# TensorE as hardware loops, with weight tiles picked by register and one semaphore for each kind of weight load

## The chip, the cores and the metric

The kernel runs on one core of a Trainium2 chip. The metric is device time in microseconds (us) of one execution. Each time below is a median of several executions. Every experiment was timed beside the kernel before, on the same chip and in the same rounds. A ratio is the mean time of one kernel's fast runs over the mean of the other's fast runs in the same rounds, so it is not quite the ratio of the quoted medians.

The engines are TensorE (PE, with weight loads as PEld), VectorE (DVE), ScalarE (ACT), GpSimd (POOL) and the sync engine that issues the loads (SP). A *unit* is one head of one batch: 128 units in all, each with a 3 MB tile of K and a 3 MB tile of V.

## The reference, cut to what matters

Two independent attention blocks decode one token against a cache, and their outputs are concatenated:

```python
B, Sq, D, H, Sk, Dh = 2, 1, 640, 32, 8192, 192          # for blocks A and B
q = (x @ wq).reshape(B, Sq, H, Dh).transpose(0, 2, 1, 3)
scores = einsum("bhqd,bhkd->bhqk", q, k_cache) * Dh ** -0.5
o = einsum("bhqk,bhkd->bhqd", softmax(scores), v_cache)
out = o.transpose(0, 2, 1, 3).reshape(B, Sq, H * Dh) @ wo
```

Everything is bfloat16. The caches make 805 MB of the 837 MB that are read, and each byte is used once.

## The kernel before

Each engine has a list of operations, each with the events it waits for. An operation stands in a *slot*, roughly the unit it belongs to. The emitter writes the list out, or, for a range of slots that repeats, as a hardware loop whose waits are computed from the turn number:

```python
lo, period, n = loop                 # slots lo .. lo + period * n - 1, as n turns
...
for fn, need, has_sig, _ in plan[:where[0]]:          # written out before the loop
    self.put(eng, fn, need, has_sig)
with eng.Fori(0, n) as i:                             # the loop
    for fn, need, has_sig, _ in body:
        self.put(eng, fn, [(sem, i * step[id(sem)] + val) for sem, val in need], has_sig)
for fn, need, has_sig, _ in plan[where[-1] + 1:]:     # written out after it
    self.put(eng, fn, need, has_sig)
```

Only VectorE and ScalarE loop, 15 turns of 8 units each; TensorE is written out in full:

```python
LOOPS = {"dve": (6, 8, 15), "act": (6, 8, 15)} if NU == 128 else {"dve": None, "act": None}
```

The loads wait for buffers. K and V have two tiles each; a K tile is free when VectorE has multiplied it, a V tile when TensorE has used it:

```python
S_sp.add(sp_k(u), waits=[key("d1b", u - NK)])         # NK = 2
S_sp.add(sp_v(u), waits=[key("pv", u - NV)])          # NV = 2
```

For each unit VectorE multiplies K by the query and sums three quarters of the products; ScalarE sums the other quarter, in 16 activations with an accumulator:

```python
for t in range(na_of(u)):                              # 16 per unit
    put(act_tab, u, 10 + t, act_acc(u, t), w, ...)
```

TensorE's work in a unit is 32 matmuls of probabilities with V. Of every four units, two add a query projection with `wq` and one an output projection with `wo`.

## Time and profile before

1972.22 us, median of 3 runs (1970.92 to 1972.57).

| Quantity | Value | View |
|---|---|---|
| Span of the profiled run | 1970.0 us | first line of the page |
| TensorE matmuls / VectorE / ScalarE busy | 57% / 84% / 46% | page, part 1 |
| Data moved | 837.52 MB | page, part 3 |
| Rate from 100 to 450 us and from 600 to 1800 us | 430 and 430 GB/s | table of stretches |
| Issue to landing of a 3 MB tile | 22.4 to 24.0 us | page, part 6 |

The page's part 2 cuts the span into 40 slices. These are the busy tenths of the 16 DMA engines, averaged over them, and the rate:

```profile
DMA  9999999999999999999999999999999999999996
GB/s 386 431 428 432 430 428 432 428 429 431 427 433 431 428 430 428 432 431 429 430 430 430 429 430 430 429 431 428 431 430 429 431 429 430 430 430 431 429 430 279
```

The DMA is full from start to tail: digit 9 in 39 of 40 slices. Part 3 lists the DMA queues: packets, MB, share of 16 engines' span.

```profile
q1 hardware_dynamic: 55856, 836.79, 99.5%
q8 instruction: 39, 0.64, 0.1%
q14 instruction: 11, 0.09, 0.0%
```

The data are q1. The other two are marked as instructions, so they are read as fetches of the engines' own programs: q8 as TensorE's (39 packets of 16 KB here), q14 as that of other engines (11 packets of 8 KB here).

Part 5 gives busy time, mean ns of one, idle time just before and what ended most of it:

```profile
L376 PE MATMUL ops<-vb,pb 128*33 128x384 bf16 x4096 | 957.5, 409 | 842.1 <-DMA vb<-in_A_v_cache_dram 364.2
...
L279 DVE TENSOR_TENSOR prodA<-kb,qbc 128x3072 bf16<-128x3072 bf16 x128 | 226.1, 1766 | 262.8 <-DMA kb<-in_B_k_cache_dram 130.2
```

Both compute engines wait for data: TensorE for V (689.0 of the 842.1 us, by the list of waits over both blocks), VectorE for K. Part 6 gives, for each kind of load, its count, KB of one and median us from issue to landing:

```profile
vb<-in_A_v_cache_dram SPq DMA_DIRECT2D x64, 3072.0 KB, 22.9
kb<-in_A_k_cache_dram SPq DMA_DIRECT2D x63, 3072.0 KB, 24.0
kb<-in_B_k_cache_dram SPq DMA_DIRECT2D x63, 3072.0 KB, 22.7
vb<-in_B_v_cache_dram SPq DMA_DIRECT2D x62, 3072.0 KB, 22.4
```

At 430 GB/s a tile takes 7.3 us, so about three tiles are under way at any time.

The trace also records each landing event: 16 separate increments of the semaphore for every 3 MB tile. The profile counts 16 DMA engines, so each increment is read here as one engine's share landing; the events carry no engine number, and this reading is the author's. The time from a tile's first increment to its last is called its *spread* below.

### The profile page before, as it was taken

Reading aid. Unit: us, or ns where it says so; the run is one execution under the profiler, and the core shown is the slowest. Engines: PE = TensorE matmul, PEld = TensorE weight load, DVE = VectorE, ACT = ScalarE, POOL = GpSimd, SP = SyncE. Lnnn points to the kernel's source line nnn. Section 1 sums busy time; section 2 is a strip of 40 time slices with the busy share of each in tenths; the row PEclk is TensorE's granted clock in tenths of the full one; section 3 lists DMA queues with packets and bytes.
Section 4 is the critical chain, followed back from the end, with each engine's and each line's share of the span. In section 5 each row is a group of like instructions: output and inputs, shape, how many; then the busy total and the mean of one; then the engine's idle time right before and its main releaser. Section 6 shows DMA issues by size and latency. Waiting matters only on the chain.

```text
span 1970.0 us, 18081 instructions
## 1 busy us (share of the span) xinstructions
PE 1118.6 (57%) x5014; PEld 593.7 (30%) x5014; DVE 1655.3 (84%) x962; ACT 904.7 (46%) x4763; POOL 113.8 (6%) x270
## 2 busy tenths in 40 slices
PE   2565556555555565555654655556655565555657
PEld 1233223323232333223332333223332233222324
DVE  7887888888888888888888888888788888888886
ACT  4444444544445444454445444444444444544454
POOL 3000000000000000000000000000000000000001
PEclk9777777777777777777777777777777777777778
DMA  9999999999999999999999999999999999999996
GB/s 386 431 428 432 430 428 432 428 429 431 427 433 431 428 430 428 432 431 429 430 430 430 429 430 430 429 431 428 431 430 429 431 429 430 430 430 431 429 430 279
DMA packets 55922, 837.52 MB, mean 425 GB/s; under 512 B 7352, under 2 KB 18240, under 8 KB 22976
## 3 DMA queue, kind: packets, MB, share of 16 engines
q1 hardware_dynamic: 55856, 836.79, 99.5%
q8 instruction: 39, 0.64, 0.1%
q14 instruction: 11, 0.09, 0.0%
q10 hardware_dynamic: 16, 0.01, 0.0%
HBM read 836.77 MB, written 0.01 MB: 425 GB/s over the span
## 4 chain that ended last, share of the span: by engine, by line
DMA 76%; DVE 17%; issue 5%; PE 1%; ACT 1%; POOL 0%; SPq 0%; ACTq 0%; DVEq 0%
DMA kb<-in_B_k_cache_dram 39%; DMA kb<-in_A_k_cache_dram 38%; DVE prodD L283 16%; ACT prodA L301 0%; DVE prodA L279 0%; PE ops L376 0%; DVE prodD L290 0%; POOL mg L266 0%; PE oTps L395 0%; PE outps L411 0%; DVE sc L294 0%; SPq L219 0%; SPq L226 0%; ACT pb L308 0%; ACT out_sb L347 0%
## 5 line engine op out<-in xcount | busy, mean ns | idle before, releaser
L376 PE MATMUL ops<-vb,pb 128*33 128x384 bf16 x4096 | 957.5, 409 | 842.1 <-DMA vb<-in_A_v_cache_dram 364.2
L376 PEld LDWEIGHTS ops<-vb,pb 128*33 128x33 bf16 x4096 | 483.3, 120 | 1316.5 <-issue 1121.0
L301 ACT ACTIVATE prodA<-prodA 128x192 bf16<-128x192 bf16 x2058 | 712.5, 351 | 118.1 <-DVE prodA L279 117.6
L283 DVE TENSOR_TENSOR prodD<-kb,qbc 128x9216 bf16<-128x9216 bf16 x128 | 632.8, 4944 | 3.5 <-DMA kb<-in_A_k_cache_dram 3.5
L290 DVE TENSOR_TENSOR prodD<-prodD 128x4608 bf16<-128x4608 bf16 (+2 forms) x384 | 598.1, 1558 | 13.3
L279 DVE TENSOR_TENSOR prodA<-kb,qbc 128x3072 bf16<-128x3072 bf16 x128 | 226.1, 1766 | 262.8 <-DMA kb<-in_B_k_cache_dram 130.2
L301 ACT ACTIVATION_READ_ACCUMULATOR prodA<-prodA 128x1 f32 x2058 | 391.3, 190 | 0.0
L305 ACT ACTIVATE nb<-mg 128x1 f32<-128x1 f32 x128 | 25.9, 203 | 701.6 <-POOL mg L266 701.6
L294 DVE TENSOR_REDUCE sc<-prodD 128x48 f32<-128x1152 bf16 x128 | 172.9, 1351 | 4.4
L266 POOL PARTITION_ALL_REDUCE mg<-mp x128 | 48.7, 381 | 1715.8 <-DVE mp L286 1715.8
L343 ACT ACTIVATE qbc<-qps 128x384 bf16<-128x384 f32 x64 | 31.4, 490 | 120.9 <-PE qps L364 120.8
L315 ACT ACTIVATE o_sb<-ops 1x384 f32<-1x384 f32 x63 | 30.1, 478 | 96.3 <-PE oTps L384 78.3
L384 PEld LDWEIGHTS oTps<-ones,o_sb 33*128 33x128 f32 x372 | 67.1, 258 | 9.8 <-issue 9.8
L384 PE MATMUL oTps<-ones,o_sb 33*128 33x1 f32 x372 | 69.8, 312 | 0.0
L270 POOL PARTITION_ALL_REDUCE lall<-rs x128 | 55.5, 434 | 114.2 <-ACT pb L308 114.2
L308 ACT ACTIVATE pb<-sc,nb 128x64 bf16<-128x64 f32 x128 | 52.2, 408 | 15.5 <-ACT nb L305 5.2
L286 DVE TENSOR_REDUCE mp<-sc 128x1 f32<-128x64 f32 x128 | 28.2, 220 | 9.9 <-ACT prodA L301 1.0
L364 PE MATMUL qps<-wqs,xbc_0 128*128 128x384 bf16 x160 | 32.4, 335 | 6.0 <-DMA wqs<-in_A_wq_dram 6.0
L364 PE MATMUL qps<-wqs,xbc_1 128*128 128x384 bf16 x160 | 32.4, 335 | 0.6 <-ACT qbc L343 0.6
L411 PE MATMUL outps<-wos,oTz 128*4 128x320 bf16 x192 | 31.2, 299 | 0.1
L316 ACT ACTIVATE o_sb<-ops 1x384 f32<-1x384 f32 x63 | 30.3, 481 | 0.7
L308 ACT ACTIVATION_READ_ACCUMULATOR pb<-sc,nb 128x1 f32 x128 | 23.8, 186 | 0.0
(30 smaller groups left out, 86.4 us busy)
## 6 DMA issues: line engine op xcount, KB each, us to landing
vb<-in_A_v_cache_dram SPq DMA_DIRECT2D x64, 3072.0 KB, 22.9
kb<-in_A_k_cache_dram SPq DMA_DIRECT2D x63, 3072.0 KB, 24.0
kb<-in_B_k_cache_dram SPq DMA_DIRECT2D x63, 3072.0 KB, 22.7
vb<-in_B_v_cache_dram SPq DMA_DIRECT2D x62, 3072.0 KB, 22.4
wos<-in_A_wo_dram SPq DMA_DIRECT2D x8, 960.0 KB, 24.5
wqs<-in_B_wq_dram SPq DMA_DIRECT2D x8, 960.0 KB, 26.8
wos<-in_B_wo_dram SPq DMA_DIRECT2D x8, 960.0 KB, 24.4
wqs<-in_A_wq_dram SPq DMA_DIRECT2D x7, 960.0 KB, 26.8
```

What stands on the lines that cost most here:

```text
L266: return lambda eng: eng.partition_all_reduce(mg[u % 2][:], mp[u % 2][:], 128, bass.bass_isa.ReduceOp.max)
L270: return lambda eng: eng.partition_all_reduce(lall[g % 2][:, b:b + 1], rs[u % 2][:], 128, bass.bass_isa.ReduceOp.add)
L279: return lambda eng: eng.tensor_tensor(prodA[u % 2][:, 0:na, :], kb[u % NK][:, 0:na, :], qb_bc(u, na), ALU.mult)
L283: return lambda eng: eng.tensor_tensor(prodD[:, 0:T - na, :], kb[u % NK][:, na:T, :], qb_bc(u, T - na), ALU.mult)
L290: return lambda eng: eng.tensor_tensor(prodD[:, 0:nd, 0:w], prodD[:, 0:nd, 0:w], prodD[:, 0:nd, w:2 * w], ALU.add)
L294: return lambda eng: eng.tensor_reduce(sc[u % 2][:, na:T], prodD[:, 0:T - na, 0:24], AXL.X, ALU.add)
L301: return lambda eng: eng.activation(prodA[u % 2][:, t, :], prodA[u % 2][:, t, :], ACTF.Identity, accum_out=sc[u % 2][:, t:t + 1])
L308: return lambda eng: eng.activation(pb[u % 2][:, :, ::32], sc[u % 2][:].rearrange("p (j a) -> p j a", a=2), ACTF.Exp, bias=nb[u % 2][:], s ...
L343: return lambda eng: eng.activation(qbc[qg % 4][:], qps[:, 0:QW].rearrange("p (a d) -> p a d", a=2), ACTF.Identity)
L364: ins = eng.matmul(qps[:, 0:QW], xbc[blk][b][:, c, :], wqs[w % 2][:, c, off:off + QW], start=(c == 0), stop=(c == DC - 1))
L376: ins = eng.matmul(ops[(u // B) % 2][0:33, b, 0:QW], pb[u % 2][:, j, :], vv[:, j, :], start=(j == 0), stop=(j == T // 2 - 1))
L384: ins = eng.matmul(oTps[:, 2 * i + b:2 * i + b + 1], o_sb[:, b, :, :].rearrange("p s (r i) -> p i (s r)", i=3)[:, i, :], ones33[:], start= ...
```

## The change

Its intent is a smaller program for TensorE: 104 of 128 units go into two loops, one per block, of 13 turns with 4 units (two heads of both batches) each. A loop body must be the same in every turn, so weight tiles move from lists of tiles into one tile with an index taken from a register, and the two semaphores of each kind of weight load become one. With one semaphore, a weight load must wait until its predecessor has been consumed; `wo` is issued a unit later, and the waits for weights move from TensorE to ScalarE. ScalarE's own loop now starts at slot 4 instead of 6; by the code, so that 15 turns end before the one copy of q that has no weight load left to wait for. The diff, cut to its core:

```diff
-        wqs = [sb(f"wqs{i}", [128, DC, HG * Dh], BF16) for i in range(2)]
-        wos = [sb(f"wos{i}", [128, HG // 2, 3, D], BF16) for i in range(2)]
+        wqs = sb("wqs", [128, 2, DC, HG * Dh], BF16)
+        wos = sb("wos", [128, HG, 3, D], BF16)
...
-            reg[("wq", w)] = (wqsem[w % 2], 16 * (w // 2 + 1))
-            reg[("wo", w)] = (wosem[w % 2], 16 * (w // 2 + 1))
+            reg[("wq", w)] = (wqsem, 16 * (w + 1))
+            reg[("wo", w)] = (wosem, 16 * (w + 1))
...
+            fn.turn = lambda it: at(bass.ds((it + pr) // npr % 2, 1), bass.ds((it + pr) % npr * QW, QW))
...
             put(act_tab, max(qg_first(qg) - 1, 0), 4 if qg_first(qg) >= 1 else -1, act_a0(qg),
-                [("pq", qg), key("d1b", qg_first(qg - 4) + 2 if qg >= 4 else -1)], ("a0", qg))
+                [("pq", qg), key("d1b", qg_first(qg - 4) + 2 if qg >= 4 else -1),
+                 ("wq", (qg + 1) // HG) if qg + 1 < NQG else None], ("a0", qg))
...
-                if u % UG == 1:
-                    S_sp.add(sp_wo(w), waits=[key("f5", ((w - 2) * HG + HG - 1) // 2 if w >= 2 else -1)])
+                if u % UG == (2 if UG >= 8 else 1):
+                    S_sp.add(sp_wo(w), waits=[key("f5", (w - 1) * HG // 2)])
...
-        LOOPS = {"dve": (6, 8, 15), "act": (6, 8, 15)} if NU == 128 else {"dve": None, "act": None}
+        LOOPS = dict(dve=[], act=[], pe=[])
+        if NU == 128 and NBLK == 2:
+            LOOPS = dict(dve=[(6, 8, 15)], act=[(4, 8, 15)], pe=[(7, 4, 13), (71, 4, 13)])
```

More of the change, by code (lines that the diff above doesn't have):

```diff
@@ L55, in put, with emit @@
             ins.then_inc(self.sem, 1)
-    def emit(self, eng, loop=None):
+    def emit(self, eng, loops=()):
         plan = self.resolve()
-        if loop is None:
-            for fn, need, has_sig, _ in plan:
-                self.put(eng, fn, need, has_sig)
-            return
-        lo, period, n = loop
-        where = [i for i, p in enumerate(plan) if p[3] is not None and lo <= p[3] < lo + period * n]
-        assert where == list(range(where[0], where[-1] + 1)) and len(where) % n == 0
-        m = len(where) // n
-        reps = [plan[where[0] + r * m:where[0] + (r + 1) * m] for r in range(n)]
-        body = reps[0]
-        step = {}
-        for r in range(1, n):
-            for a, b, c in zip(body, reps[r], reps[r - 1]):
-                assert b[3] - a[3] == r * period and a[2] == b[2]
-                assert [id(s) for s, _ in a[1]] == [id(s) for s, _ in b[1]], (self.name, a[3], b[3])
-                for (sem, v), (_, w) in zip(b[1], c[1]):
-                    assert step.setdefault(id(sem), v - w) == v - w
-        for fn, need, has_sig, _ in plan[:where[0]]:
-            self.put(eng, fn, need, has_sig)
-        with eng.Fori(0, n) as i:
-            for fn, need, has_sig, _ in body:
-                self.put(eng, fn, [(sem, i * step[id(sem)] + val) for sem, val in need], has_sig)
-        for fn, need, has_sig, _ in plan[where[-1] + 1:]:
@@ new lines, in emit @@
+        at = 0
+        for lo, period, n in loops:
+            where = [i for i, p in enumerate(plan) if p[3] is not None and lo <= p[3] < lo + period * n]
+            assert where == list(range(where[0], where[-1] + 1)) and len(where) % n == 0
+            m = len(where) // n
+            reps = [plan[where[0] + r * m:where[0] + (r + 1) * m] for r in range(n)]
+            body = reps[0]
+            step = {}
+            for r in range(1, n):
+                for a, b, c in zip(body, reps[r], reps[r - 1]):
+                    assert b[3] - a[3] == r * period and a[2] == b[2]
+                    assert [id(s) for s, _ in a[1]] == [id(s) for s, _ in b[1]], (self.name, a[3], b[3])
+                    for (sem, v), (_, w) in zip(b[1], c[1]):
+                        assert step.setdefault(id(sem), v - w) == v - w
+            for fn, need, has_sig, _ in plan[at:where[0]]:
+                self.put(eng, fn, need, has_sig)
+            with eng.Fori(0, n) as i:
+                for fn, need, has_sig, _ in body:
+                    turn = getattr(fn, "turn", None)
+                    self.put(eng, turn(i) if turn else fn,
+                             [(sem, i * step[id(sem)] + val) for sem, val in need], has_sig)
+            at = where[-1] + 1
@@ L82, in emit @@
+        for fn, need, has_sig, _ in plan[at:]:
             self.put(eng, fn, need, has_sig)
@@ L154, in build_kernel @@
         rcT = [sb(f"rcT{i}", [128, 2], F32) for i in range(2)]
-        oTz = [sb(f"oTz{i}", [128, 3, 6], BF16) for i in range(2)]
+        oTz = sb("oTz", [128, 3, 6], BF16)
         out_sb = [sb(f"out_sb{k}", [4, NH2], BF16) for k in range(NBLK)]
@@ L176, in build_kernel @@
         wq0sem = sem("wq0sem")
-        wqsem = [sem(f"wqsem{i}") for i in range(2)]
-        wosem = [sem(f"wosem{i}") for i in range(2)]
+        wqsem = sem("wqsem")
+        wosem = sem("wosem")
         xsem = [sem(f"xsem{k}") for k in range(NBLK)]
@@ L233, in sp_wq @@
             if part is None:
-                return dma(wqs[w % 2][:], src, wqsem[w % 2])
+                return dma(wqs[:, w % 2, :, :], src, wqsem)
             if part == 0:
-                return dma(wqs[w % 2][:, :, 0:QW], src[:, :, 0:QW], wqsem[w % 2])
-            return dma(wqs[w % 2][:, :, QW:HG * Dh], src[:, :, QW:HG * Dh], wq0sem)
+                return dma(wqs[:, w % 2, :, 0:QW], src[:, :, 0:QW], wqsem)
+            return dma(wqs[:, w % 2, :, QW:HG * Dh], src[:, :, QW:HG * Dh], wq0sem)
         def sp_wo(w):
@@ L242, in sp_wo @@
             src = blocks[blk]["wo"][h0 * Dh:(h0 + HG) * Dh, :].rearrange("(pr p i) n -> p pr (i n)", p=128, i=3)
-            return dma(wos[w % 2][:].rearrange("p pr i n -> p pr (i n)"), src, wosem[w % 2])
+            return dma(wos[:, (w % 2) * HG // 2:(w % 2 + 1) * HG // 2, :, :].rearrange("p pr i n -> p pr (i n)"), src, wosem)
         def sp_k(u, part=None):
@@ L336, in fn @@
                 for b in range(B):
-                    ins = eng.activation(oTz[pp % 2][:, :, 2 + b], oTps[:, b:6:2], ACTF.Identity,
+                    ins = eng.activation(oTz[:, :, 2 + b], oTps[:, b:6:2], ACTF.Identity,
                                          scale=rcT[pp % 2][:, b:b + 1])
@@ L359, in pe_p0, with at, fn @@
             w = g0 // HG
-            off = (g0 % HG) * Dh
-            def fn(eng):
-                for c in range(DC):
-                    ins = eng.matmul(qps[:, 0:QW], xbc[blk][b][:, c, :], wqs[w % 2][:, c, off:off + QW],
-                                     start=(c == 0), stop=(c == DC - 1))
-                return ins
-            return fn, [("wq", w), ("wq0b",) if (w == 0 and WQSPLIT and off >= QW) else None, ("xbc", blk),
-                        key("a0", qg - 1)]
+            npr = HG // 2
+            def at(slot, off):
+                def fn(eng):
+                    for c in range(DC):
+                        ins = eng.matmul(qps[:, 0:QW], xbc[blk][b][:, c, :],
+                                         wqs[:, slot, c, off].rearrange("p a n -> p (a n)") if slot is not w % 2 else
+                                         wqs[:, slot, c, off],
+                                         start=(c == 0), stop=(c == DC - 1))
+                    return ins
+                return fn
+            fn = at(w % 2, slice((pr % npr) * QW, (pr % npr + 1) * QW))
+            fn.turn = lambda it: at(bass.ds((it + pr) // npr % 2, 1), bass.ds((it + pr) % npr * QW, QW))
+            return fn, [("wq", w) if w == 0 else None, ("wq0b",) if (w == 0 and WQSPLIT and pr % npr >= 1) else None,
+                        ("xbc", blk), key("a0", qg - 1)]
         def pe_pv(u, j0, j1):
@@ L402, in pe_f5, with at, fn @@
             g0 = 2 * pp
+            blk = g0 // Hn
             first = (g0 % Hn == 0)
             last = (g0 % Hn == Hn - 2)
-            w = g0 // HG
-            pr = (g0 % HG) // 2
-            def fn(eng):
-                for i in range(3):
-                    for half in range(2):
-                        ins = eng.matmul(outps[g0 // Hn][0:4, 0:NH2], oTz[pp % 2][:, i, 2 - 2 * half:6 - 2 * half],
-                                         wos[w % 2][:, pr, i, half * NH2:(half + 1) * NH2],
-                                         start=(first and i == 0 and half == 0),
-                                         stop=(last and i == 2 and half == 1))
-                return ins
+            def at(pr):
+                def fn(eng):
+                    for i in range(3):
+                        for half in range(2):
+                            ins = eng.matmul(outps[blk][0:4, 0:NH2], oTz[:, i, 2 - 2 * half:6 - 2 * half],
+                                             wos[:, pr, i, half * NH2:(half + 1) * NH2],
+                                             start=(first and i == 0 and half == 0),
+                                             stop=(last and i == 2 and half == 1))
+                    return ins
+                return fn
+            fn = at(pp % HG)
+            fn.turn = lambda it: at(bass.ds((it + pp) % HG, 1))
             return fn
@@ L475, in build_kernel @@
             put(act_tab, u1 + 5 if pp == LASTP - 1 else u1 + 4, 3.5 if pp == LASTP - 1 else 3, act_f4(pp),
-                [("f3", pp), ("f2", g1 - 1), ("f2", g1), key("f5", pp - 2), ("init",)], ("f4", pp))
-            w = [("f4", pp), ("wo", (2 * pp) // HG), key("f5", pp - 1)]
+                [("f3", pp), ("f2", g1 - 1), ("f2", g1), key("f5", pp - 1), ("init",), ("wo", (2 * pp) // HG)], ("f4", pp))
+            w = [("f4", pp), key("f5", pp - 1)]
             put(pe_tab, u1 + 6 if pp == LASTP - 1 else u1 + 3, 1.2 if pp == LASTP - 1 else 2, pe_f5(pp), w, ("f5", pp))
@@ L526, in build_kernel @@
                 w = u // UG
-                if u % UG == 1:
-                    S_sp.add(sp_wo(w), waits=[key("f5", ((w - 2) * HG + HG - 1) // 2 if w >= 2 else -1)])
+                if u % UG == (2 if UG >= 8 else 1):
+                    S_sp.add(sp_wo(w), waits=[key("f5", (w - 1) * HG // 2)])
                 if u % UG == (3 if UG >= 8 else 0) and w + 1 < NWG:
-                    S_sp.add(sp_wq(w + 1), waits=[key("pq", (w - 1) * HG + HG - 1)])
+                    S_sp.add(sp_wq(w + 1), waits=[key("pq", w * HG)])
             else:
@@ L539, in build_kernel @@
             S_pool.add((lambda i: (lambda eng: eng.memset(pb[i][:], 0.0)))(i))
-        S_pool.add(lambda eng: eng.memset(oTz[0][:], 0.0))
-        S_pool.add(lambda eng: eng.memset(oTz[1][:], 0.0), sig=("init",))
+        S_pool.add(lambda eng: eng.memset(oTz[:], 0.0), sig=("init",))
         for blk in range(1, NBLK):
@@ L575, in _ @@
             def _(eng):
-                S_pe.emit(eng)
+                S_pe.emit(eng, LOOPS["pe"])
 def bass_concat_heads__gqa_block_cached__mha_block_cached__decode_kernel(
```

## The prediction

> **What bounds the kernel now.** DMA bandwidth. The page's slices show DMA at 9 in all but the last; the queue table gives the data queue 99.5% of 16 engines' span; the stretch table gives 430 GB/s from 50 to 1900 us. 837.5 MB / 430 GB/s = 1948 us; the remaining 22 us of the 1970 us span are the start (387 GB/s in the first 50 us) and the tail after the last transfer (about 1951 to 1970 us). [...]
>
> TensorE is not the limit: matmuls are busy 57% of the span, and it waits 842 us in front of the PV matmuls, 689 us of that for a V tile (list of waits). A 3 MB tile needs 7.3 us of the DMA, yet takes 22.5 to 25 us from issue to landing (issue table): about 15 us of earlier transfers are always queued when a load is issued. So a TensorE delay below some 15 us per unit postpones a V issue without emptying the queue. VectorE, 84% busy, is untouched.
>
> **What the change does.**
> - Removes: about 3/4 of TensorE's code. Each loop turn holds 4 units, 26 turns replace 104 of 128 units. The instruction queue q8 moved 39 packets, 0.64 MB. If only once-fetched code stays, about 0.45 MB less: 1.1 us of DMA at most. [...]
> - Adds on TensorE: per turn about 25 register or wait instructions and one backward branch. Estimate: at most the 170 ns gap seen between weight loads each, so under 4 us per turn[...], in a turn of about 59 us of which TensorE idles some 25. Only 11 matmuls a turn are picked by register, all short projections. None of it outlasts the DMA queue.
> - Moves: wo is issued one unit later and waits for the output projection of the previous group (first at 131.2 us, done 132.2; the queue gets there at 138.4: no wait). wq's landing is now waited for in ScalarE's copy of q: issued 153.3, landing 26.8 us later at about 180, needed about 197: 16 us early. wo lands some 60 us before ScalarE's scaled copy needs it. The single oTz buffer is reused four units later: no wait.
>
> On the critical path: only the instruction bytes; the tail is the same code.
>
> **Prediction.** 1971.0 us, 8 in 10 within 1966 to 1977. Faster by over 2%: 0.01; within 2%: 0.97; slower by over 2%: 0.02.
>
> **What the profile would show.** DMA still 9 in all slices at 430 GB/s, data bytes 836.79 MB unchanged, q8 smaller (or equal if refetched); PV's busy time about equal; idle before PV shifted from "V landing" to register/branch steps by up to 100 us in total; V issue waits for TensorE slightly later, V's issue-to-landing time shorter by the same amount; span within a few us.
>
> **What would make it wrong.** A stall at each turn above 15 us (instruction fetch behind a full DMA queue), which would show as a GB/s dip every 59 us; the issue queue blocked at wo or wq long enough to hold back K and V; or register-addressed matmuls costing microseconds each.

The sum came to 1948 us for the data and 22 us for start and tail, which is the 1970 us span (median time 1972.22 us); the forecast of 1971.0 us lies 1.2 us under that median, about the 1.1 us of instruction bytes.

## The result

| | Before | Changed |
|---|---|---|
| Median, 4 runs each | 1972.06 us | 2023.38 us |
| Range | 1970.92 to 1972.57 | 2018.97 to 2024.79 |
| Ratio (95% interval) | | 1.0257 (1.0239 to 1.0275) |

The changed kernel is 2.6% slower: "within 2%" was given 97%, and the range ended at 1977 us. The part-2 and part-3 lines of the changed kernel's page:

```profile
DMA  9999999999999999999999999999999999999995
GB/s 385 430 430 428 431 429 431 429 431 427 429 402 420 419 410 426 408 425 423 402 421 408 425 419 409 428 406 422 423 410 425 402 427 423 395 429 405 426 417 237
...
q1 hardware_dynamic: 55856, 836.79, 98.6%
q14 instruction: 81, 0.66, 0.1%
q8 instruction: 10, 0.16, 0.0%
```

Three things stand out. The data are the same 836.79 MB. TensorE's fetches fell from 39 packets to 10, as intended. But q14 rose from 11 to 81. And the rate is normal for the first 11 slices (about 550 us) and then sags, with dips to 395 to 410 GB/s. The DMA row still shows nothing: its digit 9 means 90% or more.

Both compute engines now wait longer for data, while their busy time is unchanged:

```profile
L382 PE MATMUL ops<-vb,pb 128*33 128x384 bf16 x4096 | 959.8, 410 | 890.5 <-DMA vb<-in_A_v_cache_dram 419.5
...
L279 DVE TENSOR_TENSOR prodA<-kb,qbc 128x3072 bf16<-128x3072 bf16 x128 | 226.0, 1766 | 315.3 <-DMA kb<-in_B_k_cache_dram 158.6
```

VectorE, whose program did not change, waits 315.3 us before this line instead of 262.8, nearly all of it for K: 52.5 us more, and the span grew by 51.8 us. So K comes late.

### Which program is fetched, and when

One ScalarE turn of the changed kernel lasts about 125 us. The trace has five q14 packets in each. The DMA view of 550 to 640 us holds one turn's five:

```profile
q1 hardware_dynamic: 1727, 36.78, 98.8%
q14 instruction: 5, 0.04, 0.1%
```

In the same window of the kernel before there is none from q14 and two of TensorE's:

```profile
q1 hardware_dynamic: 2002, 38.76, 100.5%
q8 instruction: 2, 0.03, 0.1%
```

Counting ScalarE's instructions at the time of each packet tells the rest. Its loop body has 338 instructions, and the five packets recur at the same places. This is the list for one turn, worked out from the trace:

```
fetch at us   ScalarE is at                           place in the 338
   428.4      near the end of the body                 297
   438.7      the backward branch                      0
   443.9      just after it                            7
   452.8      the next block                          35
   500.0      the block after it                     164
   553.3      the same place, next turn              297
```

Places 35, 164 and 297 are 129 and 133 instructions apart. One 8 KB packet would hold about 128, an estimate from q8: 0.64 MB for TensorE's 10,028 matmuls and weight loads, some 64 bytes each. A *block* below is what one 8 KB packet holds. On this estimate the body begins about 35 instructions before a block boundary, at instruction 93 of a block, and touches four blocks. Five packets come in each turn, so the fifth is taken for the block past its end; no packet says what it holds. In the kernel before, the loop begins two slots later, 74 instructions further on, at about instruction 39 of a block. Its 337 instructions end at 376 of 384 and touch three blocks. Its q14 has 11 packets in the whole span and none that recurs with the turns, so three blocks and the one after them seem to stay where they are.

### What a fetch does to the DMA engines

This is the list of landings around the first refetches of the changed kernel, again worked out from the trace. F is an 8 KB packet of q14, at its start; T is a K or V tile, at its last increment, with the last four of its 16 increments in us after its first:

```
T 188.4  1.97 1.99 2.04 3.03
F 189.8
F 195.0
T 197.1  1.97 1.99 2.04 4.38
F 203.0
T 205.0  1.98 1.99 2.05 5.06
T 212.4  1.97 2.00 2.04 5.06
T 219.7  1.96 1.99 2.05 5.06
```

Fifteen increments stay within 0.1 us of where they were; the last falls back from 3.03 to 5.06 us over three packets, some 0.69 us per packet. It is taken for the same engine each time, as its lag adds up while no other moves in this list. An 8 KB packet itself is on record with 0.31 us. Five packets put this engine an estimated 3.4 us further behind in every turn. It does not catch up between them: its lag is 5.06 us in each of the last three lines, and the DMA share is 1.01 from 100 to 450 us (table of stretches), so there is no slack to be seen. The spread is 12 us at 500 us and peaks at 15.5 us at 580 us:

| Spread, mean of 16 tiles | from 240 us on | from 480 us on | from 740 us on | from 1480 us on |
|---|---|---|---|---|
| Before | 3.0 | 3.7 | 3.9 | 7.1 |
| Changed | 6.9 | 13.0 | 12.8 | 13.1 |

The kernel waits for all 16 increments of a tile (`16 * (u // NK + 1)` in its code), so a tile counts as landed with its last one. So the pace of the kernel should be that of the one lagging engine, from the first refetch on; the sum below tests this. While the spread grows, the other engines work ahead, and the rate still reads 430 GB/s. When they are some 12 to 15 us, about two tiles, ahead, they run dry, as the author reads it, because the next load is issued only after the slowest share of an earlier tile has landed and been used, and the rate falls (417 GB/s from 600 to 1800 us). The landings fit this: between 600 and 1800 us the first share of a tile lands 10.6 us after its issue (median), down from 20.6 us between 100 and 200 us, while the last stays at about 23 us. That fits dips that begin only at 550 us.

The sum closes. Over 15 stretches of 8 units (K of unit 2 to K of unit 122), the first increments of the kernel before come every 121.43 us, its last ones every 121.97: its last shares give away 8.1 us in all. In the changed kernel the last increments come every 124.87 us in the first full turns (121.43 + 5 x 0.69 = 124.88) and every 125.7 us once the others run dry; 59.3 us in all over 15 x 121.43. 59.3 - 8.1 = 51.2, of 51.8 us that the span grew.

### The profile page after: what moved, and what is told of

The parts are those of the page before. It is cut to its first block, busy times and chain, and to the rows that moved or that the text cites. A ratio compares the mean times of both kernels' runs of the same rounds, so it can differ in the third digit from the quotient of the medians.

```text
span 2021.8 us, 18616 instructions
## 1 busy us (share of the span) xinstructions
PE 1121.5 (55%) x5014; PEld 593.6 (29%) x5014; DVE 1655.2 (82%) x962; ACT 907.5 (45%) x4763; POOL 118.8 (6%) x269
## 3 DMA queue, kind: packets, MB, share of 16 engines
q1 hardware_dynamic: 55856, 836.79, 98.6%
## 4 chain that ended last, share of the span: by engine, by line
DMA 76%; DVE 17%; issue 5%; ACT 1%; PE 1%; POOL 0%; SPq 0%; ACTq 0%; DVEq 0%
DMA kb<-in_B_k_cache_dram 39%; DMA kb<-in_A_k_cache_dram 37%; DVE prodD L283 16%; DVE prodD L290 1%; DVE prodA L279 1%; ACT prodA L301 0%; PE ops L382 0%; DVE sc L294 0%; POOL mg L266 0%; PE outps L417 0%; PE oTps L401 0%; SPq L219 0%; SPq L226 0%; ACT pb L308 0%; ACT out_sb L347 0%
## 5 line engine op out<-in xcount | busy, mean ns | idle before, releaser
L279 DVE TENSOR_TENSOR prodA<-kb,qbc 128x3072 bf16<-128x3072 bf16 x128 | 226.0, 1766 | 315.3 <-DMA kb<-in_B_k_cache_dram 158.6
L365 PE MATMUL qps<-wqs,xbc_0 128*128 (+1 forms) x160 | 32.5, 335 | 6.2 <-DMA wqs<-in_A_wq_dram 6.2
L365 PE MATMUL qps<-wqs,xbc_1 128*128 (+1 forms) x160 | 32.4, 334 | 0.6 <-ACT qbc L343 0.6
L417 PE MATMUL outps<-wos,oTz 128*4 (+1 forms) x192 | 31.8, 302 | 0.5 <-ACT oTz L337 0.5
## 6 DMA issues: line engine op xcount, KB each, us to landing
vb<-in_B_v_cache_dram SPq DMA_DIRECT2D x62, 3072.0 KB, 23.1
```

Source lines behind the costliest of these rows:

```text
L279: return lambda eng: eng.tensor_tensor(prodA[u % 2][:, 0:na, :], kb[u % NK][:, 0:na, :], qb_bc(u, na), ALU.mult)
L365: ins = eng.matmul(qps[:, 0:QW], xbc[blk][b][:, c, :], wqs[:, slot, c, off].rearrange("p a n -> p (a n)") if slot is not w % 2 else wqs[:, ...
L417: ins = eng.matmul(outps[blk][0:4, 0:NH2], oTz[:, i, 2 - 2 * half:6 - 2 * half], wos[:, pr, i, half * NH2:(half + 1) * NH2], start=(first ...
```

## The experiments

Four theories went to the chip:

1. ScalarE's loop, moved by two slots, refetches five blocks per turn; all fall on one DMA engine, which makes every tile late.
2. TensorE's loops (branches, waits computed in registers) delay the issue of V.
3. The shared semaphores and moved weight loads hold up the issue queue.
4. ScalarE itself stands still at its backward branch, and the stall, not the DMA engine, costs the time.

### Moving ScalarE's loop alone

a_act6, the changed kernel with ScalarE's loop back at slot 6 (with 14 turns, as the last `wq` wait does not repeat):

```diff
-    LOOPS = dict(dve=[(6, 8, 15)], act=[(4, 8, 15)], pe=[(7, 4, 13), (71, 4, 13)])
+    LOOPS = dict(dve=[(6, 8, 15)], act=[(6, 8, 14)], pe=[(7, 4, 13), (71, 4, 13)])
```

> The changed kernel with ScalarE's loop starting at slot 6 again (14 turns), TensorE's loops and all else kept. Theory 1 (ScalarE's loop body, moved two slots earlier, spans four 8 KB instruction blocks and refetches five per turn; all five fall on one of the 16 DMA engines, which then finishes every tile last): the refetches vanish, queue q14 falls from 81 packets to under 25, the spread of a tile's 16 partial landings stays under 5 us, time 1958 to 1972 us. Rivals 2 (TensorE's loop branches and register waits delay V issues) and 3 (the shared weight semaphores and moved weight loads hold the issue queue): 2010 to 2030 us, as the changed kernel.

Measured: 1970.33 us (5 runs), ratio 0.9991 (0.9977 to 1.0005). Its page:

```profile
GB/s 385 429 430 429 431 430 430 430 431 431 426 434 431 428 432 429 433 430 430 429 430 431 429 431 431 429 431 428 433 431 429 432 431 431 429 430 431 430 430 287
...
q14 instruction: 14, 0.11, 0.0%
```

The spread stays below 4 us up to 1800 us and ends at 5.9, a little over the stated 5; the author puts this down to fetches of the longer written-out tail after the loop (q14 has 14 packets against 11). The whole loss is gone, with TensorE's loops and the moved weight loads in place. Theories 2 and 3 fall as explanations.

b_act4, the reverse: the kernel before with nothing changed but the start of ScalarE's loop.

```diff
-        LOOPS = {"dve": (6, 8, 15), "act": (6, 8, 15)} if NU == 128 else {"dve": None, "act": None}
+        LOOPS = {"dve": (6, 8, 15), "act": (4, 8, 15)} if NU == 128 else {"dve": None, "act": None}
```

> The kernel before, with ScalarE's loop starting at slot 4 instead of 6, nothing else. Theory 1: q14 rises to about 81 packets, spread of partial landings grows by some 3.4 us per loop turn to about 15 us, time 2015 to 2030 us (no TensorE fetches saved). Rivals 2 and 3: unchanged, 1968 to 1976 us.

Measured: 2022.27 us (4 runs), ratio 1.0262 (1.0246 to 1.0278), and the spread again settles at 13 us:

```profile
GB/s 389 430 428 428 433 428 428 431 430 428 429 411 425 417 411 433 399 431 420 401 430 403 426 419 408 433 405 428 409 410 432 398 425 409 413 433 396 427 417 248
...
q14 instruction: 81, 0.66, 0.1%
```

One digit reproduces the whole loss.

### The rest of the change

a_pe_flat, the changed kernel with `pe=[]`, so TensorE is written out again:

> The changed kernel with TensorE written out again (no TensorE loops), ScalarE's loop at slot 4, weight loads as changed. Theory 1: still slow, 2015 to 2032 us, q14 about 81 packets and q8 back to 39. Rival 2: back to about 1972 us. Rival 3: about 2023 us as well.

Measured: 2024.75 us (4 runs), ratio 1.0265 (1.0250 to 1.0281). Taking TensorE's loops away does not help.

a_act6_pe_flat, with `act=[(6, 8, 14)]` and `pe=[]`:

> The changed kernel with ScalarE's loop at slot 6 and TensorE written out: what is left of the change is the weight tiles, their shared semaphores and moved loads. Theory 1: 1968 to 1976 us, q14 under 25 packets, q8 39 packets. Rival 3: about 2023 us. Beside a_act6 it gives what TensorE's loops are worth by themselves: theory 1 expects a gain of 2 to 10 us from 29 fewer 16 KB fetches.

Measured: 1972.83 us (5 runs), ratio 1.0001 (0.9987 to 1.0014). The weight tiles, semaphores and moved loads cost nothing. Between this and a_act6, of the same rounds, lie 2.5 us of medians: that is the size of the gain from TensorE's loops, at the lower end of the expected 2 to 10 us and hardly clear of the intervals.

### Shifting the loop without moving it

These keep the changed kernel's loops and put idle one-column copies into ScalarE's slots 1 to 3, so that only the address of the loop moves. The edit, for 60 copies (the others differ in the number):

```diff
-        actd = sb("actd", [128, 2], F32)
+        actd = sb("actd", [128, 62], F32)
...
+        for i in range(60):
+            put(act_tab, 1 + i % 3, 50, (lambda c: lambda eng: eng.activation(actd[:, c:c + 1], actd[:, 0:1], ACTF.Identity))(2 + i),
+                [], None)
```

> The changed kernel with 30 one-column copies put into ScalarE's slots 1 to 3, ahead of its loop: the loop's start moves from about instruction 92 to about 122 of a 128-instruction block, so its 338 instructions still touch four blocks. Theory 1: still slow, 2015 to 2030 us, q14 about 81 packets. If the padding itself helped or hurt for another reason, this and a_pad60 would move alike.

> The same with 60 copies: the loop starts at about instruction 24 of a block and touches three. Theory 1: fast, 1958 to 1974 us, q14 under 25 packets, though 30 instructions more than a_pad30. Rivals 2 and 3 (TensorE's loops, weight loads): 2015 to 2030 us.

> 88 copies ahead of ScalarE's loop: it starts at about instruction 54 of a 128-instruction block and ends at about 392, eight past the third block, so it touches four again. Theory 1: slow, 2015 to 2030 us, q14 about 81 packets, although 60 copies were fast. If padding helped because it delays or separates something, more padding should be as fast as a_pad60 (1969 us).

> 40 copies ahead of ScalarE's loop: start at about instruction 6 of a block, three blocks. Theory 1: fast, 1965 to 1971 us, q14 under 20 packets; the candidate for the faster version, 0.1 to 0.4% under the kernel before from 29 fewer TensorE fetches.

| Copies | Loop lies at instructions | Blocks | q14 packets | Median us | Ratio (interval) |
|---|---|---|---|---|---|
| 0 (changed kernel) | 93 to 431 | 4 | 81 | 2023.38 | 1.0257 (1.0239 to 1.0275) |
| 30 | 123 to 461 | 4 | 82 | 2023.80 | 1.0263 (1.0245 to 1.0280) |
| 40 | 5 to 343 | 3 | 12 | 1967.27 | 0.9979 (0.9966 to 0.9993) |
| 60 | 25 to 363 | 3 | 12 | 1968.65 | 0.9980 (0.9963 to 0.9996) |
| 88 | 53 to 391 | 4 | 82 | 2022.41 | 1.0255 (1.0239 to 1.0271) |

The second column takes the block boundary from the fetch times of the traces, good to an instruction or two, counted from the start of the block in which the loop begins. With more and more padding the kernel is slow, fast and slow again, as the number of blocks says: 391 exceeds three blocks of 128 by seven instructions. It is placement, not work, not separation in time.

### Bytes on one engine, or the stall at the branch?

a_act_flat, the changed kernel with `act=[]`: ScalarE written out, so no backward branch, but a program that still has to be fetched (44 packets, below).

> The changed kernel with ScalarE written out (no ScalarE loop). About 4900 instructions are 39 blocks of 8 KB, fetched once each without any backward branch, half of the 75 refetches. Theory 1, if every block of ScalarE's costs the same DMA engine 0.69 us: 39 x 0.69 = 27 us of lag in place of 52, so 1982 to 2002 us. Rival 4 (ScalarE's stall at the backward branch costs the time, not the bytes on one DMA engine): no branch, so 1958 to 1974 us.

Measured: 1992.06 us (4 runs), ratio 1.0102 (1.0085 to 1.0119), q14 44 packets, spread 12 us at 1450 us. There is no branch to stall at, and it is 19 us slower than the kernel before: about half the packets give two fifths of the loss. The trace of the changed kernel says the same. ScalarE's first activation after each pass of the branch waits for a result of GpSimd. It starts 0.03 us after that result in 12 of the 15 passes and 0.8 us after it in the other three, so a stall there is worth 2.3 us at most in the whole run. Theory 4 falls. It also shows that leaving a hardware loop out is no refuge here: 1992.06 us written out, 1968.65 us for the well-placed loop of a_pad60 in the same rounds.

b_row8k goes at the lag itself. No engine's program is touched but the issue queue's. To the kernel before are added 75 loads, five per 8 units, of one row of 8 KB into a spare tile:

```diff
+                if u % 8 in (0, 2, 4, 5, 7) and u >= 8:
+                    i, nrow = nrow, nrow + 1
+                    S_sp.add(dma(spare[i % 4:i % 4 + 1, :], blocks[0]["wq"][0:1, 0:4096], spsem[i % 4]), waits=[key("row", i - 4)])
```

> The kernel before with 75 added loads of one 8 KB row, 5 per 8 units, from the same issue queue[...]. No engine's program but the issue queue's is touched. Theory 1 (lag of one DMA engine): at 0.31 us (an 8 KB packet alone) to 0.69 us each, 1990 to 2028 us, with the spread of partial landings growing to 10 to 15 us. Rivals 2, 3 and 4: 0.6 MB more of 837 MB, 1971 to 1976 us.

Its data queue, against 55856 packets before:

```profile
q1 hardware_dynamic: 56006, 837.40, 99.1%
```

That is 150 packets and 0.61 MB more, two packets and 8 KB for each row: read as one packet of data and one semaphore write, and so as one DMA engine. Measured: 1987.99 us (4 runs), ratio 1.0077 (1.0060 to 1.0094). The time is 2 us under the stated range, but far from the 1971 to 1976 us of the rivals. Each row makes its engine lag by 0.32 us, about the packet's own time, and not by the 0.69 us of a program fetch: estimated from these, 75 rows make 24 us. Part of it costs nothing, as the kernel before already had a spread of 7.1 us by 1480 us, read as another engine being behind. By the sum used above, the last increments of b_row8k fall back by 23.1 us and those of the kernel before by 8.1: 15.0, of the 15.2 us measured (1987.99 - 1972.75). The spread grows to 12.8 us, as expected. 0.07% more data cost 0.8% of the time.

b_row8k_spread is its control: the same number of loads and bytes from the same places, but 16 rows of 512 bytes, meant to go one to each engine; how they were dealt out is not shown, only what became of the spread.

```diff
-                    S_sp.add(dma(spare[i % 4:i % 4 + 1, :], blocks[0]["wq"][0:1, 0:4096], spsem[i % 4]), waits=[key("row", i - 4)])
+                    S_sp.add(dma(spare[16 * (i % 4):16 * (i % 4) + 16, :], blocks[0]["wq"][0:16, 0:256], spsem[i % 4]), waits=[key("row", i - 4)])
```

> Control of b_row8k: the same 75 extra loads of 8 KB from the same queue at the same places, but as 16 rows of 512 bytes[...]. Theory 1 (lag of one engine, not bytes or issues): 1971 to 1977 us, spread of partial landings as in the kernel before. If the added issues or bytes were the cost: about 1988 us, as b_row8k.

Measured: 1976.03 us (4 runs), ratio 1.0021 (1.0005 to 1.0036), spread at most 8.3 us near 1830 us against 8.9 before. So 4.5 us (1976.03 - 1971.53 of the same rounds) are the loads themselves, and the other 11 of the 15 us of b_row8k go with the 8 KB in one row, where the spread grows to 12.8 us: on the reading above, with putting them on one engine.

### The version that beats both

a_pad40 is the changed kernel with its loop on a good address: 1967.27 us against 1971.53 us of the kernel before in the same rounds, 0.2% faster. By medians of different rounds it is 2.8% faster than the changed kernel. Its page:

```profile
GB/s 384 430 430 429 431 431 430 430 431 431 426 434 428 431 431 428 433 431 428 431 429 431 429 430 431 430 431 428 433 430 430 432 429 430 431 429 431 430 430 287
...
q1 hardware_dynamic: 55856, 836.79, 99.6%
q8 instruction: 10, 0.16, 0.0%
q14 instruction: 12, 0.10, 0.0%
```

The dips are gone. The groups of the changed kernel that waited are back at the level of the kernel before:

```profile
L382 PE MATMUL ops<-vb,pb 128*33 128x384 bf16 x4096 | 955.2, 408 | 840.1 <-DMA vb<-in_A_v_cache_dram 377.9
...
L279 DVE TENSOR_TENSOR prodA<-kb,qbc 128x3072 bf16<-128x3072 bf16 x128 | 226.3, 1768 | 258.5 <-DMA kb<-in_A_k_cache_dram 128.0
```

Its spread stays at 3.1 to 3.7 us up to 1900 us where that of the kernel before grows to 7.1 us by 1480 us, which fits TensorE's 39 fetches of 16 KB being down to 10. In the landing lists one increment falls back by some 1.0 to 1.7 us at such a fetch, but not the same one each time: in the kernel before, one goes from 3.8 to 5.3 us at the fetch of 858.6 us, and at that of 906.6 us a second one joins it at 5.4 us. So they accumulate slowly. At 1919 us of the kernel before, the increments of a tile show eight 6.7 to 8.8 us behind the first one to land and the other eight at most 3.5 us, so the 39 fetches seem to go round eight engines. By the same sum as above the last increments of a_pad40 fall back by 3.1 us instead of 8.1, which covers the 4 us.

## Why the prediction was wrong

- **"What bounds the kernel now. DMA bandwidth", 430 GB/s: right**, and shown again by a_act6 and a_pad40. But the reading was of an average. "DMA at 9" and 430 GB/s are compatible with one engine of 16 falling ever further behind; the changed kernel read 430 GB/s while it was already losing 3.4 us per turn.
- **"about 15 us of earlier transfers are always queued", so late TensorE work empties nothing: right about TensorE.** a_act6 has TensorE's loops and loses nothing. A lead of about that size, 12 to 15 us, is where the faster DMA engines run dry. Here the queue covered the late issues (a_act6, 1970.33 us); it did not cover one engine that fell 12 to 15 us behind the others (2023.38 us).
- **"Removes ... about 0.45 MB less": right.** q8 fell from 0.64 to 0.16 MB. TensorE's loop turns did not refetch.
- **"On the critical path: only the instruction bytes", worth "1.1 us of DMA at most": this is the step that failed.** It has two faults. First, it looked at TensorE's program only. It weighed refetches there, where they did not happen (q8 fell to 10 packets), while the diff plainly moved ScalarE's loop from slot 6 to slot 4; the prediction does not name this line at all. It added 70 packets. Second, it divided instruction bytes by the rate of all 16 engines. By the landing lists they fall on one engine: 0.57 MB more at 430 GB/s are 1.3 us, at a sixteenth of that rate an estimated 21 us, and they cost 51 us, because each 8 KB fetch sets its engine back by 0.69 us and not by its own 0.31.
- **"Moves: ... no wait": right.** a_act6_pe_flat, which has all moved loads and shared semaphores, is at 1.0001.
- **"What would make it wrong": none of the three.** It came nearest with fetches behind a full DMA queue, but expected the stall of an engine, seen as a dip every 59 us. The dips came with ScalarE's turns of 125 us, only after 550 us, and no engine's stall was the cause: a_act_flat has no branch and still loses 19 us.
- **TensorE's waits in front of PV**: these were to shift to register and branch steps by up to 100 us. In a_pad40 the idle time before them is 840.1 us against 842.1 before; nothing worth naming was added. The part put down to V's landing did not shrink but rose, from 689.0 to 749.1 us. V's median times from issue to landing fell from 22.9 and 22.4 us (blocks A and B) to 22.2 and 22.1.

What stays open: why a program fetch of 8 KB sets its engine back by 0.69 us when a data row of 8 KB costs 0.32 us; why ScalarE's fetches seem always to hit one DMA engine while TensorE's seem to go round eight; and why, once engines run dry, a turn costs another 0.8 us (the mean 24 KB packet then takes 936 ns in the changed kernel, between 900 and 1800 us, against 915 ns in the kernel before).

## What to carry to other kernels

Where the DMA is full, look at the last of a tile's 16 increments and not only at the mean rate. Here the rate read 430 GB/s while the spread grew to 12 us, and small transfers that, by the landing lists, fell on one engine again and again cost far more than the 1.3 to 1.4 us of their bytes at that rate: 70 more program packets, 0.57 MB, 51 us; 75 single-row loads, 0.61 MB, 15 us. Here, too, the address of a loop decided whether it was fetched again in every turn: ScalarE's 338 instructions took 1967.27 us where they touched three 8 KB blocks and 2023.80 us where they touched four. So an edit that moves code ahead of a loop can cost more than the edit; compare the packet counts of the instruction queues before and after every such change. If a count jumps, shift the loop by a few instructions and measure again.
